# A transformer block: PSUM as one pool of eight banks, value products in late bursts, side products in column tiles, bit-pattern additions on GpSimd

## The chip, the cores and the metric

The kernel runs on one NeuronCore of a Trainium2 chip. The core has five engines with queues of their own: TensorE (PE in the profile; its weight loads are PEld), VectorE (DVE), ScalarE (ACT), GpSimd (POOL) and SyncE (SP, which here only issues DMAs). They meet through semaphores. The metric is device time in microseconds (us) of one execution, the median of several.

## The reference

One block of a transformer for S = 2048 tokens of width D = 640, in bf16. Attention has 32 query heads of width 20 and one key and value head; the feed-forward part is 1536 wide.

```python
q = (LN(x) @ wq) in 32 heads of 20;  k = LN(x) @ wk;  v = LN(x) @ wv      # LN: (x - mean) / sqrt(var + 1e-5)
p = softmax(q @ k.T * 20 ** -0.5)                                        # no mask: 2048 x 2048 for each head
h = x + concat(p @ v) @ wo
h2 = h + (gelu_tanh(LN(h) @ w_gate) * (LN(h) @ w_up)) @ w_down
```

The 32 x 2048 x 2048 exponentials are 2048 tiles of 128 partitions x 512 elements.

## The kernel before, in words

**An order written at build time.** The kernel has no loop on the chip. A planner in Python (`_Plan`, lines 38 to 157, and the `decide` functions up to line 1372) goes through time with a booked cost and latency for each operation. At each step the engine that is free first chooses what to issue next, and `commit` (line 76) appends it to that engine's list with its dependencies. `resolve` and `emit` (lines 90 and 143) turn the lists into five straight instruction streams with semaphore waits. On the chip every queue runs in the order that the plan fixed; an operation that takes longer than booked holds up what is behind it on its engine, and what waits for that.

**Scores.** k is held transposed, four copies at partitions 0, 32, 64 and 96 (`kT4`), and q likewise, four heads to a group (`qT`), so a score product contracts over 32 partitions and four of them run at once in four row tiles of the array (`issue_qk`, line 880). A unit is 512 query columns of four heads (nt tiles of 128 tokens by 4/nt groups of heads); there are 32 units. For each unit and each of the 16 key tiles there is a pack: four matmuls of 512 columns, which fill four PSUM banks. Banks 0 to 5 are three fixed pairs for scores and a pack needs two free pairs (`free_groups`); banks 6 and 7 hold the accumulator of the value products and everything else.

**Exponentials.** Two engines empty the score banks. ScalarE computes exp to bf16 in `pa`, one bank (512) or two neighbouring banks (1024) per instruction (line 1212). VectorE uses a bit trick that has no table (line 1263): a * score + b, rounded to a 16-bit integer, is the bit pattern of a bf16 number near the exponential, `pd[:, 0]`. Two more patterns are that one plus 42 and plus 85 (line 1245, "chord additions", `CH_SHIFT`); the value product sums the three with weights 1, 0.793 and 0.637 (`CH_W`, stored as three scaled copies of v in `v_ext`), which evens out the error. A tile of VectorE's therefore costs one instruction from PSUM, two additions (joined for up to four neighbouring tiles, `do_adds`, line 1235) and three value products instead of one. `issue_qk` decides when it places a pack which of its tiles go to which engine.

**Value products.** (`issue_pv`, line 968.) v with a column of ones, 32 columns wide, is the weight, and the probabilities stream by: 32 x 512 results, four heads at once in four column tiles, summed in one accumulator bank over all key tiles; the ones give the softmax sum. `pe_decide` fits such rounds, and pieces of other products, into the time until the next pack's banks are expected to be free.

**Side products** are all other matmuls, full 128 x 128 (line 455): q, k and v; a transpose of the finished unit against the identity (`on_job`), after which VectorE takes the reciprocal (line 599) and multiplies (line 593); `wo`; gate, up and down. They are cut into pieces of one matmul each. The planner books `SW` = 105 ns at each change between the three ways of using the array (scores "q", values "v", side "m").

**Norms and the rest.** LN statistics, normalisation and residual sums run on VectorE (lines 367 to 435, 646, 766); the square root is a power on GpSimd (line 393); transposes of the normalised rows are DMAs from SP (line 427). For q and k the weights are first spread from 20 to 32 columns a head, by GpSimd copies (lines 326 and 332) into zeroed buffers. Gate results are copied out by VectorE (line 714) and passed through Gelu in place, three at a time (line 732), for scores are still being made and a change of ScalarE's function table takes 1283 ns; after the last exponential, Gelu is read straight from PSUM (line 716). Up results are multiplied in by VectorE (line 747). The large weights are loaded once, at about 35 us.

## Time and profile before

| | us |
|---|---|
| median of 3 runs (lowest, highest) | 851.09 (848.45, 851.84) |
| the profiled execution: its span, first to last instruction | 851.3 |
| first, last exponential of ScalarE | 24.5, 793.0 |
| busy: TensorE, VectorE, ScalarE, GpSimd | 730.3, 742.2, 763.4, 26.9 |

The time of the profiled execution outside the profiler is not given separately; its span lies within the runs shown. A group's line in the profile gives source line, engine, operation, output <- inputs with shapes, count, then busy time in us, mean duration in ns, and the idle time before such instructions with what ended it. Durations of neighbours on one engine overlap by some 0.1 to 0.2 us, so a mean duration is longer than the distance from one start to the next. Line 455 is the helper through which all side products pass, line 1212 all exponentials of ScalarE.

### The profile page before, as it was taken

What the parts mean: (1) busy time and instruction counts of PE and PEld (TensorE: products, weight loads), DVE (VectorE), ACT (ScalarE), POOL (GpSimd) and SP (SyncE); (2) the same over time, 40 slices, a digit from 0 to 9 for tenths busy, and PEclk for the clock granted to TensorE, in tenths of its full rate; (3) what the DMA queues carried; (4) which work ended last, traced back from release to release, by engine and by line L of the source; (5) the groups of instructions that cost most, each with busy time, mean ns of one, the idle gap of its engine ahead of it and who ended that gap; (6) DMA issues with size and microseconds to landing.
All of it is one profiled execution on the core that took longest, in us unless ns stands there. A gap on an engine that the chain in (4) does not pass through costs nothing.

```text
span 851.3 us, 17702 instructions
## 1 busy us (share of the span) xinstructions
PE 730.3 (86%) x6973; PEld 269.4 (32%) x6973; DVE 742.2 (87%) x1856; ACT 763.4 (90%) x1070; POOL 26.9 (3%) x60
## 2 busy tenths in 40 slices
PE   0877778778889989999998998999999999898998
PEld 0522222222222222233332222223333333232587
DVE  7768988987898989999999998999999999899533
ACT  0779999999999999999999999999999999999322
POOL 5300000000000000000000000000000000000000
PEclk9969979996898999999999998999999999999999
DMA  6780000100000000000021000000102000000100
GB/s 180 144 283 1 16 2 9 10 1 1 7 12 16 1 2 1 2 1 8 27 31 32 2 1 1 2 1 2 39 2 55 2 2 17 17 9 9 32 17 33
DMA packets 42930, 21.84 MB, mean 26 GB/s; under 512 B 34016, under 2 KB 41568, under 8 KB 42848
## 3 DMA queue, kind: packets, MB, share of 16 engines
q1 hardware_dynamic: 40224, 19.83, 9.6%
q8 instruction: 57, 0.93, 0.5%
q10 hardware_dynamic: 2624, 0.87, 0.5%
q14 instruction: 25, 0.20, 0.1%
HBM read 10.21 MB, written 2.62 MB: 15 GB/s over the span
## 4 chain that ended last, share of the span: by engine, by line
ACT 66%; PE 20%; DVE 10%; DMA 3%; issue 1%; SPq 0%; DVEq 0%
ACT pa L1212 64%; PE ps L455 11%; PE ps L968 5%; PE ps L880 5%; DVE pd L1263 4%; DVE pd L1245 2%; ACT gbuf L732 1%; DMA xn1T<-xn_tmp 1%; DMA xh<-in_A_x_dram 1%; DVE stats L374 1%; DVE stats L367 1%; DMA onT<-onq 0%; DVE xn_tmp L435 0%; DVE xh L646 0%; ACT L1212 0%
## 5 line engine op out<-in xcount | busy, mean ns | idle before, releaser
L1212 ACT ACTIVATE pa<-ps 128x512 bf16<-128x512 f32 (+1 forms) x1006 | 722.1, 935 | 21.4 <-PE ps L880 20.7
L1263 DVE TENSOR_SCALAR pd<-ps 128x512 uint16<-128x512 f32 x520 | 355.2, 687 | 48.4 <-PE ps L880 40.7
L968 PE MATMUL ps<-pd,v_ext 128*32 128x512 bf16 x1560 | 280.3, 405 | 21.3 <-ACT pa L1212 14.1
L968 PE MATMUL ps<-pa,v_ext 128*32 128x512 bf16 x1528 | 272.2, 404 | 11.8 <-ACT pa L1212 8.0
L880 PE MATMUL ps<-qT,kT 32*128 32x512 bf16 x2048 | 211.4, 401 | 53.9 <-ACT pa L1212 26.0
L1245 DVE TENSOR_SCALAR pd<-pd 128x512 uint16<-128x512 uint16 (+2 forms) x832 | 230.2, 319 | 8.8
L880 PEld LDWEIGHTS ps<-qT,kT 32*128 32x128 bf16 x2048 | 57.9, 91 | 229.5 <-DVE pd L1263 195.1
L968 PEld LDWEIGHTS ps<-pd,v_ext 128*32 128x32 bf16 x1560 | 67.2, 95 | 110.1 <-issue 47.9
L968 PEld LDWEIGHTS ps<-pa,v_ext 128*32 128x32 bf16 x1528 | 66.1, 94 | 92.4 <-issue 42.0
L455 PE MATMUL ps<-xn2T,wu_sb 128*128 128x512 bf16 (+2 forms) x360 | 69.0, 317 | 6.0 <-DVE gbuf L747 5.9
L455 PE MATMUL ps<-xn2T,wg_sb 128*128 128x512 bf16 (+2 forms) x360 | 68.1, 311 | 0.0
L455 PE MATMUL ps<-xn1T,wq_pad 128*128 128x128 bf16 (+2 forms) x320 | 47.9, 288 | 21.1 <-DMA xn1T<-xn_tmp 20.3
L455 PE MATMUL ps<-wd_sb,gbuf 128*128 128x320 bf16 x384 | 59.6, 300 | 0.0
L747 DVE TENSOR_TENSOR gbuf<-ps,gbuf 128x512 bf16<-128x512 f32 (+2 forms) x72 | 36.5, 509 | 18.3 <-PE ps L455 11.9
L716 ACT ACTIVATE gbuf<-ps 128x128 bf16<-128x128 f32 (+1 forms) x36 | 11.2, 312 | 38.1 <-PE ps L455 38.1
L455 PEld LDWEIGHTS ps<-wd_sb,gbuf 128*128 128x128 bf16 x384 | 34.3, 98 | 20.9 <-issue 8.1
L455 PEld LDWEIGHTS ps<-xn2T,wu_sb 128*128 128x128 bf16 x360 | 26.6, 99 | 32.3 <-issue 14.3
L393 POOL TENSOR_TENSOR ln_denb<-ln_veb,halfc 128x2 bf16<-128x2 bf16 (+1 forms) x19 | 12.6, 673 | 749.1 <-DVE ln_veb L389 749.1
L455 PEld LDWEIGHTS ps<-xn1T,wq_pad 128*128 128x128 bf16 x320 | 23.2, 103 | 39.8 <-DMA xn1T<-xn_tmp 20.3
L455 PEld LDWEIGHTS ps<-xn2T,wg_sb 128*128 128x128 bf16 x360 | 25.8, 98 | 25.1 <-issue 14.7
L766 DVE TENSOR_TENSOR xh<-xh,ps 128x320 bf16<-128x320 bf16 x32 | 15.4, 482 | 17.4 <-PE ps L455 17.4
L455 PE MATMUL ps<-wo_sb,onT 128*128 128x320 bf16 x160 | 28.3, 301 | 0.1
(47 smaller groups left out, 266.2 us busy)
## 6 DMA issues: line engine op xcount, KB each, us to landing
out_dram<-xh SPq DMA_DIRECT2D x16, 160.0 KB, 1.8
xh<-in_A_x_dram SPq DMA_DIRECT2D x3, 640.0 KB, 9.9
wg_sb<-in_B_w_gate_dram SPq DMA_DIRECT2D x1, 1920.0 KB, 8.9
wu_sb<-in_B_w_up_dram SPq DMA_DIRECT2D x1, 1920.0 KB, 10.2
wd_sb<-in_B_w_down_dram SPq DMA_DIRECT2D x1, 1920.0 KB, 14.0
gbuf<-in_A_wq_dram ACTq DMA_DIRECT2D x2, 400.0 KB, 8.3
wo_sb<-in_A_wo_dram SPq DMA_DIRECT2D x1, 800.0 KB, 5.3
xh<-in_A_x_dram SPq DMA_DIRECT2D x2, 160.0 KB, 2.8
```

The source lines that it names most:

```text
L367: dve(lambda e: e.bn_stats(stats[:, ln, t, 6:12], xh[:, t, HALF:D]), 356, [key], [("st", ln, t, 1)], prio, c)
L374: dve(lambda e: e.bn_stats(stats[:, ln, t, 0:6], xh[:, t, 0:HALF]), 356, [key], [("st", ln, t, 0)], prio, b)
L393: task(("pool",), lambda e: e.tensor_tensor(ln_denb[:, ln, sl], ln_veb[:, ln, sl], halfc[:, 0:n], ALU.pow), 1010, L_POOL, [("veb", kk), "h ...
L455: return lambda e, b: e.matmul(o(b), l, r, start=st, stop=sp, **kw)
L716: task(("act",), lambda e: e.activation(o, bank(bk, n), ACT.Gelu_apprx_tanh), ("gelu", c_act(n)), L_ACT, [("b", bk)], gkeys(b, fc), 1.0, fin2)
L747: dve(lambda e: e.tensor_tensor(o, bank(bk, n), o, ALU.mult), c_dve(n), [("b", bk)] + gkeys(b, fc), gkeys(b, fc), 1.0, fin)
L766: dve(lambda e: e.tensor_tensor(xh[:, t, h * HALF:(h + 1) * HALF], xh[:, t, h * HALF:(h + 1) * HALF], bank(bk, HALF), ALU.add), c_dve(HALF ...
L880: ins = e.matmul(bank(b), kT4[32 * r:32 * r + 32, kt * P:(kt + 1) * P], qT[32 * r:32 * r + 32, s, :], start=True, stop=True, tile_position ...
L968: ins = e.matmul(ps[32 * r:32 * r + 32, ab * 512:(ab + 1) * 512], v_ext[:, it["kt"], it["w"], :], it["ap"], start=st, stop=(j in ends), ti ...
L1212: op = plan.commit("act", lambda e: e.activation(dst, src, ACT.Exp, scale=SM_SCALE), cost, L_ACT, [("b", b0 + i) for i in range(n)], [("pa ...
L1245: op = plan.commit("dve", (lambda w, a: lambda e: e.tensor_scalar(pd[:, w, a], pd[:, 0, a], float(CH_SHIFT[w]), None, ALU.add))(w, a), k * ...
L1263: op = plan.commit("dve", lambda e: e.tensor_scalar(pd[:, 0, s * 512:(s + 1) * 512], bank(b), CH_A, CH_B, ALU.mult, ALU.add), c_dve(512), ...
```

## The change

Most of the planner's decisions and several operations are rewritten:

- **Units of 256 columns.** There are 64 units of 256 query columns; a pack takes two key tiles and has eight matmuls of 256 columns and 20 contracted rows (two key tiles by four heads), again four banks. q is still computed for 512 columns, for two units at once.
- **One pool of banks.** Any four free banks of the eight take a pack (five, if other work is ready and holds none), and a pack whose last banks come free within 250 ns may be issued in parts. Tiles go into one list, `tiles_q`, and ScalarE and VectorE each take from it when they are free; ScalarE takes two at once only if four are ready and two are neighbours. VectorE takes at most 4 tiles of a unit and head in the first 16 units and 3 later (`quota0`, `quota`).
- **Late burst.** A unit gets its accumulator bank only when 14 rounds of value products are ready (`open_r`), or all are, or buffers run short; the rounds then run in bursts of up to 6. `pa` grows from 16 to 26 tiles, `pd` from 8 to 9.
- **Column tiles.** Every side product is issued as four matmuls of 32 output columns at four column positions, the way that value products use the array; the planner books no change between the two.
- **GpSimd.** Both additions go to GpSimd, as 64-bit integer additions of a constant that holds the shift four times, for one tile or two neighbours. They may begin only when the power operations of the first norm are done. The second norm's square root is computed on VectorE instead, by three Newton steps of tiny instructions.
- **Smaller edits.** q and k weights are used unspread, reading 32 columns from a 20-column step. The scaled copies of v are made from PSUM by ScalarE or VectorE. The finished pair of units is transposed by a DMA from SP (`onu`) and not by TensorE. First-norm work has the highest priority on VectorE. Gate copies and outputs may go to ScalarE too. A batch of the feed-forward part waits only for earlier batches that use the same columns of `gbuf`. x is loaded in smaller parts over two queues.

The core of the diff:

```diff
-    NA = 16
-    ND = 8
+    NA = PRM["NA"]
+    ND = PRM["ND"]
...
-    def mm(o, l, r, st, sp, **kw):
-        return lambda e, b: e.matmul(o(b), l, r, start=st, stop=sp, **kw)
+    def mm(o, l, r, st, sp):
+        def fn(e, b):
+            ins = None
+            for q in range(4):
+                ins = e.matmul(o(b)[32 * q:32 * q + 32], l(q), r, start=st, stop=sp, tile_position=(0, 32 * q))
+            return ins
+        return fn
...
-                ins = e.matmul(bank(b), kT4[32 * r:32 * r + 32, kt * P:(kt + 1) * P], qT[32 * r:32 * r + 32, s, :],
-                               start=True, stop=True, tile_position=(32 * r, 0))
+                for h in range(2):
+                    kt = 2 * kp + h
+                    for r, b in part:
+                        ins = e.matmul(ps[:, b * 512 + h * 256:b * 512 + h * 256 + 256],
+                                       kT4[32 * r:32 * r + Dh, kt * P:(kt + 1) * P],
+                                       qT[32 * r:32 * r + Dh, s, hq * 256:hq * 256 + 256],
+                                       start=True, stop=True, tile_position=(32 * r, 0))
...
-                ins = e.matmul(ps[32 * r:32 * r + 32, ab * 512:(ab + 1) * 512], v_ext[:, it["kt"], it["w"], :],
+                ins = e.matmul(ps[32 * r:32 * r + 32, ab * 512:ab * 512 + 256], v_ext[:, it["kt"], it["w"], :],
                                it["ap"], start=st, stop=(j in ends), tile_position=(0, 32 * r))
...
-            op = plan.commit("dve", (lambda w, a: lambda e: e.tensor_scalar(
-                pd[:, w, a], pd[:, 0, a], float(CH_SHIFT[w]), None, ALU.add))(w, a), k * 512 / 3.84 + 60.0, L_DVE,
+                a = slice(s0 * 128, (s0 + k) * 128)
+                sh = CH_SHIFT[w] * 0x0001000100010001
+                op = plan.commit("pool", (lambda w, a, sh: lambda e: e.int64_add(
+                    pd64[:, w, a], pd64[:, 0, a], sh))(w, a, sh), k * 128 * 1.7 + 180.0, L_POOL,
                 [("pd", 0, s0 + i) for i in range(k)], [("pd", w, s0 + i) for i in range(k)], at=t)
...
+    def pick_bank():
+        return min(free_now, key=lambda b: (((b - 1) in free_now) + ((b + 1) in free_now), b))
...
+        if cand and len(free_now) >= need:
...
+            issue_qk(t, cand[0], cand[1], best[1])
             return True
...
+        rd = [x for x in ready_tiles(t) if x["u"]["nd"][x["r"]] < (PRM["quota0"] if x["u"]["id"] < PRM["quota_n"] else PRM["quota"])]
+        if rd and dve_ok() and pool_load < PRM["pool_max"] and \
+                plan.ready("dve", (), [("pd", w, pd_next[0]) for w in range(3)]) <= t + 20:
```

Instructions of the two programs:

| | before | after |
|---|---|---|
| matmuls: scores, values, side | 2048, 3088, 1837 | 4096, 7140, 7156 |
| exponentials of ScalarE: 1024 wide, 512 wide | 522, 484 | 167, 953 |
| VectorE: tiles from PSUM, additions | 520, 832 | 761, 0 |
| GpSimd: additions of one tile, of two | 0, 0 | 1282, 120 |
| changes of tiling on TensorE | 1272 | 970 |

## The prediction, made before the changed kernel was run

> **What bounds the kernel now.** I read the busy times first, then the costliest groups (shapes kept apart), the busy time by stage, and the list of waits.

> ```profile
> PE 730.3 (86%) x6973; PEld 269.4 (32%) x6973; DVE 742.2 (87%) x1856; ACT 763.4 (90%) x1070; POOL 26.9 (3%) x60
> ...
> ACT 66%; PE 20%; DVE 10%; DMA 3%; issue 1%; SPq 0%; DVEq 0%
> ```

> The chain that ended last is two thirds ScalarE. The groups say with what:

> ```profile
> L1212 ACT ACTIVATE pa<-ps 128x1024 bf16<-128x1024 f32 x522 | 590.4, 1140 | 4.8 <-PE ps L880 4.5 <-PE ps L968 0.2
> L1263 DVE TENSOR_SCALAR pd<-ps 128x512 uint16<-128x512 f32 x520 | 355.2, 687 | 48.4 <-PE ps L880 40.7
> L1212 ACT ACTIVATE pa<-ps 128x512 bf16<-128x512 f32 x484 | 345.8, 714 | 16.6 <-PE ps L880 16.1
> ...
> L1245 DVE TENSOR_SCALAR pd<-pd 128x512 uint16<-128x512 uint16 x650 | 157.8, 285 | 6.1
> ...
> L332 POOL COPY wq_pad<-gbuf 128x400 bf16<-128x400 bf16 x8 | 3.8, 520 | 4.3 <-DMA gbuf<-in_A_wq_dram 4.3
> ```

> ScalarE exponentiates 2 x 522 + 484 = 1528 of the 2048 score tiles, VectorE 520. The two exp groups together are busy 722.1 us and idle before themselves only 21. Their mean durations overlap, so I use the distance from start to start of back-to-back ones in the trace: 486 ns (512 wide) and 916 ns (1024 wide) in the mean; 484 x 0.486 + 522 x 0.916 = 713, which meets 722. For VectorE's tile it is 605 ns, for its 512-wide addition 205.

> ```profile
> 24.00:100.00 76.00, 59.24 (x627) 24.11 (x623) 60.83 (x167) 65.37 (x88) 7.33 (x20) 0.87 0.43 118
> 100.00:793.00 693.00, 611.95 (x5736) 196.46 (x5736) 641.62 (x1564) 682.45 (x940) 6.06 (x9) 0.96 0.05 10
> 793.00:851.00 58.00, 55.42 (x576) 45.19 (x574) 23.71 (x64) 13.13 (x38) 0.56 (x1) 1.00 0.13 30
> ```

> (Stage, its length, busy PE, PEld, DVE, ACT, POOL, granted clock, DMA share, GB/s.) The first exp starts at 24.5 us and the last ends at 793: a score stage of 769 us, in which ScalarE is busy 748, or 97%. Then come 58 us of feed-forward work that TensorE sets.

> ```profile
> PEld ps L880 <- DVE pd L1263: 195.1, 421, 1.3
> ...
> ACT pa L1212 <- PE ps L880: 20.7, 32, 3.8
> ```

> The next four score products wait for a bank that an exponential has not yet freed; ScalarE hardly waits. So TensorE's idleness is an effect, and the score stage is worth what ScalarE is relieved of, until another engine fills up.

> I sum against the profiled execution, whose span is 851.3 us; the runs' median is 851.09 (848.45 to 851.84), so nothing of size lies around the span. A difference under 0.5% (4.3 us) cannot be told from no change.

> **Part by part.** Counts are from the order of instructions in the two programs.

> *ScalarE.* Exponentials become 953 single and 167 double (1287 tiles, so VectorE takes 761): 953 x 0.486 + 167 x 0.916 = 616 us. The 12 Gelu runs (16.8) and six table loads (7.7) stay; evacuations that it now shares (9 gate copies, 16 outputs of 256 columns, 5 q, some 18 small) are about 16. Sum in the score stage 656, against 749 before: 93 less. At the old filling of 97.4% the stage would last 674.

> *VectorE.* 761 x 0.605 = 460. The 832 additions go (650 x 0.205 + 166 x 0.342 + some 10 = 200). The other work, norms, up products, residual adds, copies, 117 tiny Newton instructions at about 75 ns, is about 149 inside the stage. Sum 609: 88% of 694.

> *GpSimd.* 1282 additions of one tile and 120 of two, each tile as 128 integers of 8 bytes. No row shows this instruction. Low bound: the COPY above starts every 462 ns for 400 elements, 1.155 ns each; 256 four-byte words make 296 ns. High bound: two of GpSimd's 40-element TENSOR_SCALARs (line 491, 348 ns each) stand in 0.68 us, so 330 ns from start to start; that plus 256 words is 626 for one tile, 920 for two. The first is nearer in kind (one operand in, one out), but an addition in software is more than a copy, so I take 420 and 700: 1282 x 0.42 + 120 x 0.70 = 622 us; at the ends 450 and 913. It runs beside the rest from about 36 us (first addition now) until some 60 us before the end, so at 622 it is covered, at 90% of its room. What it adds is a wait: the product rounds with the second and third weight wait for it, TensorE's queue is in order, the next score product stands behind them, and ScalarE behind that. [...]

> [...]

> *TensorE.* Score products: 512 packs of 8 x 256 columns. A 256-column matmul follows the last after 109 ns, four row tiles at once: 512 x 0.219 = 112. Value products: 7140 of 256 columns, four column tiles at once, 1785 rounds x 0.109 = 195 (before 772 x 0.216 = 167). Side products are cut in four column tiles; the columns streamed stay: 222 us in all, of which some 41 fall to the tail and 3 to the head. Changes of tiling: now 1272 at about 99 ns lost each = 126; after, side and value products share a tiling and 970 are left = 96. Sum in the stage 112 + 195 + 178 + 96 = 581; the same sum for before is 574. TensorE is relieved of nothing.

> What the rows do not show is the rate of instructions: 18,392 pairs of weight load and matmul in place of 6973. Densest known:

> ```profile
> 28.00 0.40 PE L455 MATMUL ps<-wv_sb,xn1T 128*128 128x20 bf16 x10
> ...
> 841.15 0.72 PE L455 MATMUL ps<-xn2T,wg_sb 128*128 128x128 bf16 x10
> ```

> The first are 25 ns apart, for ten only; the second line is one of a long run at 55.6 ns. At 25 ns all pairs take 460 us and hide; at 55.6 they take 1023. The long run is at its streaming time, so it sets no floor; four tiles of a round start 3 ns apart. I take 25 as nearest.

> *All eight banks, late burst.* No instruction's time; it sets how much of ScalarE's waiting stays. Bounds for the stage: ScalarE never waits, 656; TensorE keeps its idle time of now, 769 - 574 = 195, and the stage is 581 + 195 = 776. I take ScalarE at 94.5%, so 694: nearer the first, since the idle time is waiting for exponentials, yet below the present 97.4%, because four engines now stand at 84 to 94% in a fixed order.

> *Head.* The chain of x loads, norm and transpose to the first product (20.3 us) stays; GpSimd's q and k padding went beside it. 24 us.

> *Tail.* After the last value product 96 down groups at 136 ns instead of 192, 119 at 109, 240 at 56, 10 at 136: 41 instead of 54. The output transpose through SP (2.5 us to landing, as its other transposes show) replaces four matmuls (0.4): +2. 58 - 13 + 2 = 47. If four small column tiles cost 4 x 25 ns instead of 56, +11. The 32 transposes themselves (1.4 us of SP's queue each, 45 in all) stand ahead of x2 transposes and stores on a queue mostly empty; nothing.

> [...] The trace has four 32-column loads starting 3 ns apart beside running matmuls, but only with 512 columns to hide them.

> Sum: 24 + 694 + 47 = **765 us**.

> **Rivals.**
> *GpSimd binds (slower).* Place: the additions on GpSimd. 36 + additions + 60 passes 851 when they exceed 755 us, that is from 504 ns a tile. At the high bound 36 + 913 + 60 = 1009; at 510 ns it is 860. For: its TENSOR_SCALAR of 40 elements already costs 330. Against: COPY.
> *TensorE's issue binds (slower).* From 45 ns a pair, 18,392 pairs fill the present time; at 50 they give 20 + 920 = 940. For: no dense run of more than ten pairs under 55 ns. Against: 3 ns inside a round.
> *The gain goes into bank waits.* 24 + 776 + 47 = 847, no change within the measurement; in part, 800 to 845. For: the 195 us row. Against: that row names exponentials.

> **Numbers.** Forecast (727 to 800) 0.60; bank waits 0.16 (0.12 still faster, 0.04 the same); GpSimd 0.14; issue 0.10. So faster 0.72, same 0.04, slower 0.24. The low end is 24 + 656 + 47 = 727; the high end takes in the bank waits and GpSimd up to 510 ns, 862; beyond lie some 0.18.

> **What will show it.** Right: exps x1120 near 616 us busy, ScalarE over 90% in the score stage; GpSimd's addition near 0.4 us and GpSimd under 92% busy. Wrong: value products (line 975) idle behind the line of the GpSimd additions, a tile over 0.5 us; TensorE's 256-column rounds over 130 ns apart; ScalarE idle behind score products for over 60 us; or a tail over 55 us.

## The result, and the profile after

The changed kernel takes 822.03 us in the median of four runs (816.63 to 823.53), the kernel before 851.47 beside it (848.45 to 856.65): a ratio of 0.9625, 95% interval 0.9576 to 0.9674. Faster, by 29 us where 86 were forecast. The profiled execution has a span of 821.2 us; the sums below are made against it.

The page's busy times, and its chain by engine:

```profile
PE 737.2 (90%) x18392; PEld 408.6 (50%) x18392; DVE 678.4 (83%) x1389; ACT 699.3 (85%) x1231; POOL 567.9 (69%) x1424
...
PE 47%; DVE 31%; ACT 13%; issue 4%; DMA 3%; POOL 2%; SPq 0%; POOLq 0%
```

ScalarE was two thirds of the chain and is 13% of it now; TensorE has taken its place with 47%, VectorE follows with 31%. No engine is full: they stand at 90, 83, 85 and 69%.

The costliest groups (shapes joined):

```profile
L1266 ACT ACTIVATE pa<-ps 128x512 bf16<-128x512 f32 (+1 forms) x1120 | 649.3, 694 | 55.9 <-PE ps L912 43.6
L1405 POOL INT64_ADD pd<-pd x1402 | 560.5, 419 | 170.9 <-DVE pd L1325 153.2
L1325 DVE TENSOR_SCALAR pd<-ps 128x512 uint16<-128x512 f32 x761 | 484.9, 681 | 72.7 <-PE ps L912 63.7
```

The exponentials are the 1120 that were counted. GpSimd's additions take 0.42 us in the mean; told apart by the order, 0.40 us for one tile and 0.62 for two, where 0.42 and 0.70 had been taken. GpSimd itself waits 171 us, nearly all of it for VectorE. What is new is the idle time behind line 912, the score products: 44 us of ScalarE's and 64 of VectorE's, against 21 and 41 before.

The four stages (stage, its length, busy PE, PEld, DVE, ACT, POOL, granted clock, DMA share, GB/s). The first exponential starts at 20.1 us, the last ends at 764.0:

```profile
20.13:100.00 79.87, 65.87 (x1564) 35.31 (x1561) 54.58 (x128) 65.52 (x116) 44.81 (x107) 0.77 0.48 116
100.00:340.00 240.00, 217.50 (x4720) 109.56 (x4714) 210.35 (x412) 217.07 (x374) 188.23 (x454) 0.92 0.10 16
340.00:763.97 423.97, 405.36 (x10040) 219.70 (x10035) 380.90 (x737) 401.15 (x695) 330.23 (x847) 1.00 0.10 20
763.97:821.20 57.23, 44.06 (x1867) 39.93 (x1864) 21.04 (x68) 12.54 (x38) 0.00 (x0) 0.99 0.11 27
```

Head 20, score stage 744, tail 57: the forecast was 24, 694 and 47. The clock column is to be noted: 0.77 and 0.92 up to 340 us, 1.00 from there on.

**The trace against the order's own times.** Each instruction is in the planner's list with a booked start, and the chip runs every queue in that order, so the two can be laid side by side, instruction by instruction (VectorE has 1389 in both). I call chip start minus booked start the slip. It is worked out from the trace and the program; the profile does not print it. In the changed kernel it grows by 30.2 us between 20 and 340 us, by only 2.8 from there to the last exponential, and by 12 in the tail. The planner books the score stage at 710.8 us, so 744 = 711 + 33. Before, the stage was booked at 745.9 and took 769: it slipped by 16.1 up to 340 us, 6.3 later, and by nothing in the tail.

Three things are therefore to be explained: why the order itself has 711 us and not the forecast's 694; why the chip falls behind it in the first 340 us; and why the tail has 57 us and not 47.

**The tail** shows its cause in a timeline. TensorE's weight loads from 790.5 us on (start, length, group, count; in brackets the idle time before it and its releaser):

```profile
791.30 0.45 PEld L502 LDWEIGHTS ps<-xn2T,wg_sb 128*32 128x32 bf16 x30 [1.62 <-issue]
791.66 0.65 PEld L502 LDWEIGHTS ps<-xn2T,wu_sb 128*32 128x32 bf16 x40
792.22 0.65 PEld L502 LDWEIGHTS ps<-xn2T,wg_sb 128*32 128x32 bf16 x40
792.78 0.35 PEld L502 LDWEIGHTS ps<-xn2T,wu_sb 128*32 128x32 bf16 x18
795.05 0.34 PEld L502 LDWEIGHTS ps<-xn2T,wu_sb 128*32 128x32 bf16 x22 [1.92 <-issue]
795.29 0.65 PEld L502 LDWEIGHTS ps<-xn2T,wg_sb 128*32 128x32 bf16 x40
795.85 0.65 PEld L502 LDWEIGHTS ps<-xn2T,wu_sb 128*32 128x32 bf16 x40
796.41 0.43 PEld L502 LDWEIGHTS ps<-xn2T,wg_sb 128*32 128x32 bf16 x25
798.40 0.23 PEld L502 LDWEIGHTS ps<-xn2T,wg_sb 128*32 128x32 bf16 x15 [1.56 <-issue]
```

Forty loads (ten column-tiled products) take 0.56 us, so four column tiles stream in 56 ns, as booked. But 30 + 40 + 40 + 18 = 128 loads, with their 128 matmuls, are 256 instructions; then TensorE stands for 1.6 to 1.9 us without waiting for anything. Counted from the program's start, every such gap of the tail falls on the same place in a block of 256, to within one instruction. A block arrives every 3.35 to 3.75 us, which is 26 to 29 ns for a weight load and its matmul. The page's list of DMA queues (packets, MB, share) counts this instruction fetch too, first of the changed kernel, then of the kernel before:

```profile
q8 instruction: 146, 2.39, 1.2%
```

```profile
q8 instruction: 57, 0.93, 0.5%
```

That is 16.4 KB a packet, and 89 packets more for 22,838 more loads and matmuls: 257 to a packet.

**The first 340 us.** The half-clock stretches in the trace are 3.41 us long or a multiple of it (13 of them up to 340 us, of 3.41 to 13.65 us). Five neighbouring windows of 3.41 us, with the same columns as above:

```profile
110.56:113.97 3.41, 3.41 (x106) 2.31 (x99) 1.76 (x5) 3.41 (x7) 2.08 (x6) 1.00 0.03 5
113.97:117.38 3.41, 3.20 (x70) 1.37 (x66) 3.34 (x6) 3.06 (x6) 2.47 (x7) 1.00 0.02 5
117.38:120.80 3.42, 2.71 (x40) 0.92 (x34) 3.42 (x7) 3.42 (x7) 3.40 (x10) 1.00 0.00 0
120.80:124.21 3.41, 3.18 (x59) 1.70 (x56) 1.50 (x3) 2.21 (x4) 2.85 (x7) 0.51 0.03 7
124.21:127.62 3.41, 3.19 (x80) 1.39 (x72) 3.16 (x6) 3.05 (x6) 2.26 (x6) 0.99 0.00 0
```

The window with only 40 matmuls is followed by one at half clock. For each window I add up the columns that its matmuls streamed, each weighted by the share of the array that its tile holds, and divide by the columns that fit at full clock, 8192 at some 0.42 ns each (512 follow one another in 215 to 216 ns in the kernel before); this is TensorE's **use**. In the five windows it is 0.77, 0.50, 0.27, 0.44 and 0.56. In the 14 traces of this case, up to 800 us and without the first eight windows, 193 windows at full clock had a use below 0.40, and 150 of them were followed by half clock; of the 2631 at or above 0.40, 15 were. The edge is not sharp: below 0.34 half clock followed 104 of 109 windows, from 0.44 on none, and in between both happen. So TensorE is slowed for having too little to do, not too much. In the first 340 us there are fewer side products beside scores and values (71 of 320 us of TensorE's time, against 171 of 424 in the rest of the stage), and the value products come in bursts: this is where the low windows lie.

I call half of the time spent at half clock the clock lost: 37.5 us between 20 and 340 us after, 32.4 before.

### The profile page after: what moved, and what is told of

It reads as the page before. It is cut to its first block, busy times and chain, and to the rows that moved or that the text cites. A ratio compares the mean times of both kernels' runs of the same rounds, so it can differ in the third digit from the quotient of the medians.

```text
span 821.2 us, 41718 instructions
## 1 busy us (share of the span) xinstructions
PE 737.2 (90%) x18392; PEld 408.6 (50%) x18392; DVE 678.4 (83%) x1389; ACT 699.3 (85%) x1231; POOL 567.9 (69%) x1424
## 4 chain that ended last, share of the span: by engine, by line
PE 47%; DVE 31%; ACT 13%; issue 4%; DMA 3%; POOL 2%; SPq 0%; POOLq 0%
DVE pd L1325 22%; PE ps L502 18%; PE ps L975 16%; PE ps L912 12%; ACT pa L1266 10%; POOL pd L1405 1%; ACT gbuf L764 1%; DMA onu<-osb 1%; DVE onq L634 1%; DMA xn2T<-xn_tmp 1%; DVE qT L378 1%; DVE gbuf L779 1%; DMA onT<-onq 1%; DVE osb L1011 1%; DVE stats L385 1%
## 5 line engine op out<-in xcount | busy, mean ns | idle before, releaser
L1266 ACT ACTIVATE pa<-ps 128x512 bf16<-128x512 f32 (+1 forms) x1120 | 649.3, 694 | 55.9 <-PE ps L912 43.6
L1405 POOL INT64_ADD pd<-pd x1402 | 560.5, 419 | 170.9 <-DVE pd L1325 153.2
L1325 DVE TENSOR_SCALAR pd<-ps 128x512 uint16<-128x512 f32 x761 | 484.9, 681 | 72.7 <-PE ps L912 63.7
L975 PE MATMUL ps<-pd,v_ext 128*32 128x256 bf16 x4566 | 276.6, 286 | 9.1 <-DVE pd L1325 4.1
L912 PE MATMUL ps<-qT,kT 20*128 20x256 bf16 x4096 | 248.3, 281 | 34.0 <-DVE pd L1325 18.1
L975 PE MATMUL ps<-pa,v_ext 128*32 128x256 bf16 x2574 | 234.1, 288 | 4.1 <-ACT pa L1266 1.4
L975 PEld LDWEIGHTS ps<-pd,v_ext 128*32 128x32 bf16 x4566 | 163.5, 99 | 66.3 <-issue 31.4
L912 PEld LDWEIGHTS ps<-qT,kT 20*128 20x128 bf16 x4096 | 81.0, 93 | 195.5 <-DVE pd L1325 103.3
L502 PE MATMUL ps<-xn2T,wu_sb 128*32 128x512 bf16 (+2 forms) x1440 | 70.6, 312 | 5.4 <-issue 5.2
L502 PE MATMUL ps<-xn2T,wg_sb 128*32 128x512 bf16 (+2 forms) x1440 | 70.1, 309 | 5.3 <-issue 4.6
L779 DVE TENSOR_TENSOR gbuf<-ps,gbuf 128x512 bf16<-128x512 f32 (+2 forms) x72 | 36.4, 508 | 25.7 <-PE ps L502 16.1
L502 PEld LDWEIGHTS ps<-wd_sb,gbuf 128*32 128x32 bf16 x1536 | 39.2, 96 | 16.6 <-issue 9.6
```

Of the source, the lines that this page charges most:

```text
L502: ins = e.matmul(o(b)[32 * q:32 * q + 32], l(q), r, start=st, stop=sp, tile_position=(0, 32 * q))
L779: dve(lambda e: e.tensor_tensor(o, bank(bk, n), o, ALU.mult), c_dve(n), [("b", bk)] + gkeys(b, fc), gkeys(b, fc), 0.8, fin)
L912: ins = e.matmul(ps[:, b * 512 + h * 256:b * 512 + h * 256 + 256], kT4[32 * r:32 * r + Dh, kt * P:(kt + 1) * P], qT[32 * r:32 * r + Dh, s, ...
L975: ins = e.matmul(ps[32 * r:32 * r + 32, ab * 512:ab * 512 + 256], v_ext[:, it["kt"], it["w"], :], it["ap"], start=st, stop=(j in ends), ti ...
L1266: op = plan.commit("act", lambda e: e.activation(dst, src, ACT.Exp, scale=SM_SCALE), cost, L_ACT, [("b", b0 + i) for i in range(n)], [("pa ...
L1325: op = plan.commit("dve", lambda e: e.tensor_scalar(pd[:, 0, s * 512:(s + 1) * 512], bank(b), CH_A, CH_B, ALU.mult, ALU.add), c_dve(512), ...
```

## The experiments

When the first four were designed, the theory was: order (17 us), half clock (most of 33), instruction fetch (10). The rivals were that TensorE's work binds the whole stage, that bank turns arise on the chip, and that GpSimd's additions are waited for. Each kernel is the changed kernel with the edit shown, unless it says otherwise; where the order is kept, the planner's list and all waits are the same. The kernel before, run beside them, had medians of 851.2 to 853.1 us.

| kernel | median (lowest, highest) | clock | booked end | stage | tail | clock lost, slip, 20 to 340 us |
|---|---|---|---|---|---|---|
| before | 851.5 (848.5, 856.7) | 0.956 | 824.8 | 769 | 58 | 32.4, 16.1 |
| after | 822.0 (816.6, 823.5) | 0.954 | 769.4 | 744 | 57 | 37.5, 30.2 |
| t128 | 813.3 (803.4, 818.7) | 0.949 | 769.4 | 745 | 45 | 37.5, 27.8 |
| t64 | 812.0 (808.5, 818.2) | 0.946 | 769.4 | 748 | 45 | 41.0, 32.0 |
| smalladd | 815.3 (808.2, 815.7) | 0.950 | 769.5 | 737 | 57 | 37.5, 24.7 |
| nochord | 822.2 (819.7, 825.8) | 0.925 | 769.4 | 739 | 57 | 54.6, 27.5 |
| fill | 802.0 (799.2, 803.2) | 0.983 | 776.3 | 733 | 47 | 10.2, 14.3 |
| noextra | 830.4 (824.3, 835.4) | 0.869 | 745.4 | 753 | 49 | 78.5, 36.8 |
| dveadd | 894.8 (892.6, 896.6) | 0.902 | 825.9 | 818 | 55 | 64.9, 35.8 |
| open4 | 878.1 (874.5, 883.3) | 0.943 | 819.4 | 722 | 131 | 25.6, 14.1 |
| allfull | 810.2 (807.7, 818.3) | 0.960 | 769.4 | 743 | 44 | 29.0, 23.2 |
| tuned | 795.9 (791.0, 800.3) | 0.965 | 755.0 | 726 | 43 | 23.9, 20.2 |
| tunedfill | 788.4 (786.6, 790.4) | 0.989 | 752.3 | 725 | 40 | 6.8, 15.1 |
| bfill | 848.9 (847.4, 850.0) | 0.990 | 830.2 | 763 | 61 | 5.1, 8.2 |

Clock, stage, tail, clock lost and slip are those of the profiled execution, which is one of the runs; the profiled one of tuned and of tunedfill is the fastest of its four.

### t128 and t64: the tail with fewer, wider tiles, order kept

```diff
-            for q in range(4):
-                ins = e.matmul(o(b)[32 * q:32 * q + 32], l(q), r, start=st, stop=sp, tile_position=(0, 32 * q))
+            ins, n = None, 128 if tl and getattr(l, "wide", 0) else 32
+            for q in range(0, 128, n):
+                ins = e.matmul(o(b)[q:q + n], l(q // 32, n), r, start=st, stop=sp, **({} if n == 128 else dict(tile_position=(0, q))))
```

(`tl` is set for a job that starts after the last exponential; t64 has 64 in place of 128.)

> Side products that start after the last exponential (feed-forward of the last batch) are issued as one full 128-column matmul in place of four column tiles: 461 matmuls instead of 1844; order, waits and everything before stay. Theory (TensorE gets its instructions in blocks of 256, each about 3.4 to 3.75 us, so 27 ns for a weight load and its matmul; four column tiles of 128 columns stream in 56 ns but bring four pairs, 108 ns): the tail falls from 57 us to 47 to 49, the gaps marked issue at every 256th instruction vanish from it, total 812 to 814. Rival (the tail is set by VectorE's and ScalarE's emptying of banks, or by Gelu): tail 55 to 57, total 820 to 823.

> The same with two tiles of 64 columns: 922 matmuls instead of 1844 in the tail. Fetch theory: two pairs take 2 x 27 = 54 ns, just under the 56 ns that 128 columns stream, so the gain is nearly all there: tail 47 to 50, total 812 to 815. Rival (each column tile costs some time of its own, whatever the supply of instructions): half the gain, tail 52 to 53, total 817 to 818.

The tails of t128 and of t64 (windows, columns as above):

```profile
765.90:810.90 45.00, 41.91 (x486) 35.27 (x481) 21.02 (x68) 12.48 (x38) 0.02 (x1) 1.00 0.11 30
```

```profile
771.20:816.40 45.20, 42.01 (x945) 38.32 (x942) 21.01 (x68) 12.41 (x37) 0.00 (x0) 1.00 0.12 31
```

Both 45 us, 12 less than with column tiles, with 486, 945 and 1867 matmuls for the same work; the medians are 9 and 10 us lower. In the list of waits of the tail the changed kernel has two rows of which the others have only the first, at 0.2 us:

```profile
PEld ps L502 <- issue: 12.7, 12, 1.9
PE ps L502 <- issue: 10.2, 9, 1.8
```

So the supply of instructions is what costs the 12 us. A cost of each tile of its own would have left t64 half way.

### smalladd: GpSimd's additions cut to 8 integers, order kept but for one pair of tiles

```diff
-                    pd64[:, w, a], pd64[:, 0, a], sh))(w, a, sh), k * 128 * 1.7 + 180.0, L_POOL,
+                    pd64[:, w, a.start:a.start + 8], pd64[:, 0, a.start:a.start + 8], sh))(w, a, sh), k * 128 * 1.7 + 180.0, L_POOL,
```

> GpSimd's additions work on 8 integers instead of 128 for a tile or 256 for two, and the value products with the second and third weight read the unshifted pattern: nearly all of the additions' work is left out, their places, waits and the order stay. Theory (the order holds the pace at full clock, TensorE's clock costs the first 300 us): no more than 5 us, total 817 to 824, GpSimd's busy time far lower. Rival (value products wait for GpSimd, 25 us in the list of waits, and score products behind them): 15 to 25 us, total 797 to 807.

815.3, 7 us below the changed kernel: a little more than the 5 allowed, far from the 15 to 25 of the rival. GpSimd's busy time fell from 568 to 268 us, and the slip up to 340 us from 30.2 to 24.7 at the same clock lost. The waits of value products for GpSimd are real and cost a few us; they are not where the gain went.

### nochord: TensorE relieved of 80 us, order kept

```diff
-            for j, (r, ab, it, st, u) in enumerate(calls):
+            for j, (r, ab, it, st, u) in [x for x in enumerate(calls) if x[1][2]["w"] == 0 or x[1][3] or x[0] in ends] or [(0, calls[0])]:
```

> Left out: 2927 of the 3044 value products with the second and third weight (those that open or close a sum, or stand alone, stay); everything else, order and waits included, is as it was. That is 732 rounds x 0.109 = 80 us of TensorE. Theory (at full clock the fixed order of the other engines sets the pace; at reduced clock TensorE falls behind the order): the slip against the order in the first 340 us, 30 us in all, falls to under 15, after 340 us little changes; total 797 to 812. Rival 1 (TensorE binds the whole score stage): most of the 80 us, total 742 to 765. Rival 2 (turns of banks between ScalarE and VectorE, TensorE has no part in it): under 4 us, 818 to 823.

822.2: nothing gained. By its numbers this is rival 2, and the theory's forecast failed. But the granted clock is the surprise: 0.915 to 0.931 in the four runs, against 0.942 to 0.962 of the changed kernel. The stretch from 20 to 340 us, first of the changed kernel, then of nochord:

```profile
20.00:340.00 320.00, 283.51 (x6280) 144.99 (x6278) 265.06 (x539) 282.59 (x489) 233.17 (x561) 0.88 0.20 41
```

```profile
20.00:340.00 320.00, 281.57 (x5232) 130.79 (x5228) 268.29 (x548) 284.65 (x500) 234.44 (x563) 0.83 0.20 42
```

A thousand matmuls fewer, and TensorE busy nearly as long: its clock went from 0.88 to 0.83, which is 17 us more of clock lost, against some 29 us that the missing matmuls would have streamed. From this I formed the theory of the use per window, counted it in the traces, and put it to the test from the other side.

### fill: TensorE given more to do

```diff
+        fb = pick_bank() if free_now else None
+        if cand and fb is not None and state["npack"] < 256 and ("xn1T", 1) in plan.w and plan.ready("pe", [("xn1T", 0), ("xn1T", 1)], ()) <= t:
+            w0 = sum(max(0.0, min(o.end, t) - max(o.t0, t - 3400.0)) for o in plan.ops["pe"][-60:])
+            if w0 < 0.8 * 3400.0 and t + 110.0 + swv + 40.0 <= lim:
...
+                        ins = e.matmul(ps[32 * q:32 * q + 32, c0:c0 + 256], xn1T[:, 0, 32 * q:32 * q + 32],
+                                       xn1T[:, 0, 0:256], start=True, stop=True, tile_position=(0, 32 * q))
```

> The t128 kernel, with 183 rounds of four extra matmuls (128 x 32 weights, 256 columns, into a bank that is free at that moment, never read) put by the planner where TensorE would stand idle and has been busy under 80% of the last 3.4 us, within the first half of the score stage. The planner books an end at 776.3 us instead of 769.4. Theory (TensorE runs at half clock in stretches of 3.41 us or multiples, each after a stretch of 3.41 us in which its array streamed less than about 0.4 of the time; half clock is what makes the chip fall behind the order in the first 340 us, 28 us in t128): the clock lost before 340 us falls from 38 us to under 12, the slip from 28 to under 14, the total from 813 to 800 to 806, granted clock over 0.975. Rival (the clock does not follow TensorE's use, or the slip has another cause): the extra rounds only cost, total 815 to 822, clock 0.95.

802.0 (ratio to before 0.9414, interval 0.9378 to 0.9451): 11 us less than t128, with 183 rounds of useless matmuls more and an order booked 7 us longer. The runs of the two do not overlap, but only just (799.2 to 803.2, 803.4 to 818.7). The stretch of t128, then of fill:

```profile
20.00:340.00 320.00, 285.70 (x6396) 147.04 (x6389) 267.34 (x545) 284.32 (x498) 236.01 (x563) 0.88 0.21 42
```

```profile
20.00:340.00 320.00, 293.41 (x7299) 159.89 (x7290) 275.00 (x549) 291.68 (x504) 244.77 (x589) 0.97 0.19 41
```

The clock of the stretch is 0.97 and all engines get more done in the same 320 us: 7299 matmuls instead of 6396 (at most 732 of them fillers), ScalarE 504 instructions instead of 498. The slip is 14.3 instead of 27.8, for 27 us less of clock lost: 0.5 us for each. So the half clock is a cause of the slip, of some 13 us here; a part of these may be slack, since the order with the fillers is booked 7 us longer.

The runs of one kernel, whose order is one and the same, point the same way. The changed kernel took 816.6 us at a clock of 0.962 and 823.5 at 0.942, tuned (below) 791.0 at 0.965 and 800.3 at 0.951: 16 and 11 us more of clock lost for 7 and 9 us.

### noextra: the products of nochord left out, and the order made anew

```diff
-        u["todo"] += 4
+        u["todo"] += 0
...
-        u["out"][r] += 1
+        u["out"][r] -= 1
...
-            u["out"][r] -= 1
-            item(w, op)
+            fr(); fr()
```

> Left out: all value products with the second and third weight, and this time the planner knows it, so the order is made anew (3044 matmuls, 761 rounds, 83 us of TensorE less; GpSimd's additions stay, nobody reads them). The planner books an end at 745.4 us instead of 769.4. Theory (the chip runs the order as booked, apart from the clock's half-speed stretches and the end; the order is bound by TensorE together with the other engines): 24 us less from the order, no less slip, total 795 to 803. Rival (nochord showed no gain, so TensorE has no part in the pace at all): 815 to 823.

830.4 (824.3 to 835.4), against 795 to 803 expected and 815 to 823 by the rival: slower than the changed kernel, with 83 us less of TensorE's work and an order booked 24 us shorter. Both were wrong, as neither reckoned with a clock that falls further with less work:

```profile
20.00:340.00 320.00, 272.23 (x5052) 115.82 (x5048) 271.67 (x546) 279.42 (x472) 233.61 (x529) 0.75 0.19 41
340.00:740.00 400.00, 363.82 (x7808) 169.15 (x7804) 356.92 (x679) 374.51 (x675) 308.65 (x782) 0.94 0.10 19
```

0.75 up to 340 us, 0.94 after: 104 us of clock lost, 56 of slip. The 24 us gained in the order were paid back, and 8 more.

### dveadd and open4: one part undone each

```diff
-                op = plan.commit("pool", (lambda w, a, sh: lambda e: e.int64_add(
-                    pd64[:, w, a], pd64[:, 0, a], sh))(w, a, sh), k * 128 * 1.7 + 180.0, L_POOL,
+                op = plan.commit("dve", (lambda w, a: lambda e: e.tensor_scalar(
+                    pd[:, w, a], pd[:, 0, a], float(CH_SHIFT[w]), None, ALU.add))(w, a), k * 512 / 3.84 + 60.0, L_DVE,
```

> Undoes one part: the additions go back to VectorE, as 16-bit additions for up to four neighbouring tiles, when four wait or slots are short; all else of the change stays, the order is made anew (booked end 825.9 us). Theory (of the change's parts only the move of the additions to GpSimd pays; without it VectorE fills up): slower than before, 860 to 880. Rival (the pool of eight banks and the late burst bring most of the gain): 825 to 845.

894.8 (ratio 1.0507, interval 1.0467 to 1.0547). Without the move to GpSimd the rest of the change, with the planner's constants as they are, is 43 us slower than the kernel before; the move is worth 73 us here, more than all that was gained. The planner had already shifted tiles back: VectorE takes 654 instead of 761. The busy times of dveadd:

```profile
PE 783.5 (88%) x17964; PEld 420.4 (47%) x17964; DVE 802.0 (90%) x2017; ACT 752.7 (84%) x1220; POOL 7.4 (1%) x22
```

VectorE is the fullest engine. The time lies 15 us above the range; the order was booked as expected, but with a clock of 0.902 the stage slipped by 49 us instead of 33.

```diff
-    "early": 530.0, "slack": 60.0, "open_r": 14, "press_a": 5, "press_d": 2, "v_min": 2,
+    "early": 530.0, "slack": 60.0, "open_r": 4, "press_a": 5, "press_d": 2, "v_min": 2,
```

> Undoes the late burst alone: a unit gets its accumulator bank from 4 ready rounds on instead of 14; the order is made anew (booked end 819.4 us). Theory (an accumulator held longer takes one of the eight banks from the scores): total 860 to 875, slower than before. Rival (banks are not what is short): 818 to 830.

878.1 (ratio 1.0317, 1.0262 to 1.0372), 3 us above what was expected and not for the reason given. Its stage and tail:

```profile
20.90:743.30 722.40, 647.48 (x14786) 314.31 (x14779) 630.00 (x1232) 658.57 (x1168) 560.13 (x1322) 0.93 0.14 28
743.30:874.20 130.90, 116.70 (x3485) 84.86 (x3482) 45.44 (x108) 26.49 (x59) 0.00 (x0) 0.98 0.08 22
```

The score stage is not longer but shorter, 722 us. The tail is 74 us longer: side products are left for the end, where no exponentials run beside them (3485 matmuls after the last exponential, against 1867). The order itself has it so, for the planner books 118 us after the last exponential instead of 45. The likely reason is that an accumulator held longer takes the bank of the side products; no view shows who holds the banks. A short tail is what the late burst buys.

### allfull: no column tiles for the side products but q and k, order kept

```diff
-            for q in range(4):
-                ins = e.matmul(o(b)[32 * q:32 * q + 32], l(q), r, start=st, stop=sp, tile_position=(0, 32 * q))
+            ins, n = None, 128 if 1 and getattr(l, "wide", 0) else 32
+            for q in range(0, 128, n):
+                ins = e.matmul(o(b)[q:q + n], l(q // 32, n), r, start=st, stop=sp, **({} if n == 128 else dict(tile_position=(0, q))))
```

> Undoes the column tiles of the side products, except q and k, whose unspread weights need them: 1344 full 128-column matmuls instead of 5376 column tiles; the order, the waits and all else stay as in the changed kernel. Changes of tiling on TensorE rise from 970 to 1147, which the planner has not booked. Theory (the column tiles save the 177 changes at about 99 ns, 17 us of TensorE in the score stage, of which the order can hide about half, and cost 10 to 12 us of instruction fetch at the end): 812 to 822, the tail 47 instead of 57. Rival (the added changes of tiling fall fully on the pace): 825 to 832.

810.2: 12 us faster than the changed kernel, as t128, and a little under the range. The stage is as long with the 177 more changes of tiling (743 us against 744). This execution lost 8.5 us less of clock up to 340 us, though, and after 340 us it slipped by 9.2 us, where the changed kernel slipped by 2.7 and t128 by 6.2: a cost of a few us may be hidden. On the whole the column tiles of these side products were a loss, and the loss lies at the end.

### tuned, tunedfill and bfill

```diff
-    "early": 530.0, "slack": 60.0, "open_r": 14, "press_a": 5, "press_d": 2, "v_min": 2,
-    "q_ahead": 2, "lay": 0, "flex_d": 400.0, "pair_min": 4, "age": 3000.0, "pool_max": 3000.0,
-    "stag_n": 3, "stag_w": 250.0,
+    "early": 400.0, "slack": 60.0, "open_r": 13, "press_a": 5, "press_d": 3, "v_min": 3,
+    "q_ahead": 2, "lay": 0, "flex_d": 600.0, "pair_min": 5, "age": 3000.0, "pool_max": 4000.0,
+    "stag_n": 3, "stag_w": 300.0,
...
-    "rate": 350.0, "w_tol0": 0.0, "w_max0": 2, "lag": 20, "quota0": 4, "quota_n": 16,
+    "rate": 300.0, "w_tol0": 200.0, "w_max0": 2, "lag": 20, "quota0": 4, "quota_n": 32,
...
-    SW = 106.0
+    SW = 104.0
```

(and `w_max` 3, `w_tol` 800, fourteen constants in all; both on t128's tail. tunedfill has fill's rounds besides; bfill has the like in the kernel before.)

> The t128 kernel with 11 of the planner's constants changed (accumulator opened at 13 rounds, early 400, pairs of tiles from five ready ones, 32 units with the larger share for VectorE, change of tiling booked at 104 and so on), no operation of another kind or size; the order is made anew and booked to end at 755.0 us instead of 769.4. Theory (what the score stage lost against the forecast at full clock lies in the order itself, and the chip runs what is booked): 14 us below t128's 813, so 796 to 803. Rival (the waits arise on the chip, whatever the order): 810 to 818.

> The same constants with the filler rounds of the fill kernel (114 of them, through the first 300 packs), booked to end at 752.3 us. Theory: both gains add up: slip of the score stage 14 to 18 us instead of 28 to 34, total 778 to 787, granted clock over 0.97. Rival (the two gains are one and the same): 795 to 802.

> The kernel before the change with 245 such filler rounds in the first 256 packs, booked to end at 830.2 us instead of 824.8. Theory (before, ScalarE set the pace and TensorE at half clock was mostly hidden, 16 us of slip for 32 us of clock lost): the clock rises over 0.97, the slip falls by 8 to 12 us, the order costs 5, total 843 to 849, a smaller gain than the 11 us in the changed kernel. Rival (half clock costs the same in both kernels): 836 to 842.

tuned takes 795.9, 17 us less than t128 for 14 booked: the operations are of the same kinds, VectorE takes 790 tiles instead of 761, and the stage fell by 19. Of these 19, 12 are booked (700 us instead of 711), and 9 of the 12 are work that ScalarE no longer has (634 us booked in the stage instead of 642); ScalarE's booked share stays at 90 to 91%. The other 7 are smaller slip up to 340 us, with 14 us less of clock lost.

tunedfill takes 788.4 (ratio 0.9253, interval 0.9213 to 0.9294), faster than both kernels of this case by 63 and 34 us, but just outside the 778 to 787 expected; the filler's gain is smaller on this order, 7.5 us. The slip of its stage was to be 14 to 18 us and is 26.6, as large as tuned's 26.8: up to 340 us it is 5 smaller, for 17 us less of clock lost (0.3 us for each), and after that 5 larger (11.4 instead of 6.5), at a granted clock of 1.00. So the two gains add up only in part.

bfill takes 848.9 (ratio 0.9959, 0.994 to 0.9978), 3 us less: the clock lost fell by 27 us, the slip by 8 (0.3 us for each), and the order's 5 us took most of that back.

## Why the prediction was wrong

The direction and the mechanism were right: additions off VectorE, tiles off ScalarE, GpSimd covered. The size was not. Of 56 us missed (821 against 765), the head gave 4 back, the stage took 50 and the tail 10.

- **ScalarE's work** was right: 1120 exponentials; back to back they start every 487 and 917 ns in the mean (486 and 916 were taken), 617 us for 616. The row shows 649 us busy, not near 616: 904 of the 1120 are overlapped by what follows them, against 958 of 1006 before, and one that stands alone counts for its whole length.
- **"I take ScalarE at 94.5%, so 694"** is the step that failed: 744. With the same 656 us of work ScalarE stands at 88% of the stage (92% by the busy times of the rows). The bounds given with it, 656 and 776, held. It took the share at which an engine stands as a small correction to the one that binds. Of the 50 us, 17 are in the order: the planner itself filled ScalarE to no more than 656 / 711 = 92%. That packs, bursts and side products have to be fitted around eight banks is the likely reason, and not shown; tuned shortens the stage mostly by giving ScalarE less work, not by filling it better. The other 33 are slip.
- **Slip.** The forecast had none of its own. In the kernel before, the chip was 16 us late up to 340 us, 8 of them with the half clock (bfill), and this was inside the 97.4% of ScalarE that I started from. Of the changed kernel's 30 us up to 340 us some 13 go with the half clock (fill) and some 5 with the waits for GpSimd (smalladd); the rest is open. Each us of clock lost cost 0.5 us in fill against t128, 0.3 in bfill against before and 0.3 in tunedfill against tuned, so it is not shown that half clock costs more in the changed kernel. I had read the clock column, 0.87 and 0.96 in the first two stages, and made nothing of it.
- **"I take 25 as nearest"** (ns for a weight load and its matmul) was right for the stage, where rounds of 256 columns come 109 to 110 ns apart, and wrong for the tail, where the +11 us that the working named and did not take came true. The tail is 57 us, where 47 were forecast and over 55 was named as a sign of being wrong, and 45 without the dense stream.
- **GpSimd** at 420 and 700 ns was 400 and 617, 560 us in all for 622; that its addition costs more than a copy was an estimate, and start to start it took 376 ns where the copy's rate gave 296; the waits behind it cost a few us (smalladd, 7). **VectorE** at 605 ns was 600. **Changes of tiling** fell as counted, but saved at most a few us (allfull).
- **The late burst** was left to the bank waits. It decides the tail, not the stage (open4), and the forecast had no term for that.
- **The rivals.** GpSimd did not bind, nor the rate of instructions over the whole program. "The gain goes into bank waits, in part 800 to 845" holds the number. As waits that arise on the chip it does not hold, for at full clock the changed kernel keeps to its order within 3 us over 424; how much of the order's own 17 us is waiting for banks is not shown.

Measured from start to start, the addition for one tile takes 376 ns on GpSimd and took 205 on VectorE. That it costs more there was outweighed by VectorE's lack of time, and dveadd puts the size to it: 73 us. On GpSimd a second tile adds 217 ns, and the rest of the 400 is near the 200 ns that smalladd's additions of 8 integers take.

Left open: the slip in the first 340 us that remains with little clock lost (14 us in fill, 15 in tunedfill, 8 in bfill), 4 to 12 us after it in several runs, and why the order fills ScalarE no further.

## What to carry to other kernels

An engine that waits little can be relieved only as far as the next ones have room; with three engines at 87 to 93% of a stage in a fixed order, work out the stage from the order's own booked times and allow for slip, instead of taking a share of one engine. Look at the clock column by stage before trusting any TensorE time: work taken off TensorE may be paid back in clock (noextra: 83 us less of it, 8 us slower), and an idle slot filled with matmuls that nobody reads can be worth more than the slot (fill: 11 us faster). Count instructions where they are densest, not in the mean (the tail: 12 us).
